# Four small edits to the order of an adaLN block: the MLP gate's sum and turn, b2's place, one pair's maxima, one group order

## The chip, the cores and the metric

The kernel runs on one core of a Trainium2 chip. The time is device microseconds of one execution; a measurement is the median of several executions. A profile is one more execution, recorded by the hardware profiler; its times are microseconds from the first instruction, and a line such as L1149 is a line of the kernel before the change. Engines are called by the names of the profile: PE (TensorE), DVE (VectorE), ACT (ScalarE), POOL (GpSimd) and SP (SyncE, which here only issues DMAs).

## What is computed

A transformer block on 2048 rows of 640 numbers, whose two halves are scaled, shifted and gated by six rows `mod` that are made from one vector `c`:

```python
mod = (silu(c) @ w_mod).reshape(1, 6, 1, 640)
sa, ca, ga, sb, cb, gb = (mod[:, i] for i in range(6))
h = layernorm(x) * (1 + ca) + sa
x = x + ga * attention(h)            # linear attention, 32 heads of 20, feature map softmax(pq), softmax(-pq)
h = layernorm(x) * (1 + cb) + sb
x = x + gb * (relu(h @ w1 + b1) ** 2 @ w2 + b2)
```

In attention each head's q and k go through a 20 x 20 matrix and two softmaxes (one of the values, one of their negatives); `kv` and `z` are sums over all rows, and the output is `phi_q kv / phi_q z`, times `wo`. The row `gb`, the MLP's gate, and its product with `b2` are what one of the edits touches.

## The kernel before, in words

The 2048 rows are 16 tiles of 128, or 8 pairs. Three stages follow each other. The first (to about 250 us) makes q, k and v of all tiles, the sums `kv` and `z`, and, on the side, the rows of `mod`. The second (about 250 to 389 us) is a loop over the 8 pairs, `for j in range(NB)`, and makes the attention's output; the sixth column of `mod`, the gate `gb`, is finished in it. The third (from 389 us) is the MLP, again pair by pair (`j`) and in seven steps (`n`) of two feature blocks (`f`).

Products are split in high and low parts: `hi` is a copy on ACT that rounds, the low part is the rest, subtracted on DVE (helper `lo`, L88), and a product is three matmuls, high by high, high by low, low by high (helper `three`, called by `mm`, L78).

The order of the second stage is written out by hand for PE, DVE, ACT and POOL (`tc.manual_schedule`): on each of these engines instructions stand in the order in which the code issues them. The order of SP's DMAs is left to the scheduler in this stage; in the MLP's first pair it is written by hand too. In one turn `j` of the second stage:

- `e_prod`, `e_recip` and `e_scale` (L877 to L906) make the scaled features of the tiles 2j+5 and 2j+6, or nearly so: two long DVE products with a sum between them, and small steps on POOL and DVE.
- `do_wo(j, i, h)` (PE tiles `pwo`) multiplies the output of pair j, in high and low parts `ot`, by `wo`: for each of two tiles (i) and two column ranges (h, 384 and 256 wide) 16 matmuls, of which the third is the first that reads a low part.
- `tr_e(j + 1, gs)` (PE `te`, ACT `ept`) transposes the features of the next pair in six groups: 0 to 4 of 120 columns in two halves, 5 of 80 columns. They go in two calls, groups 0, 1, 2 and then 5, 3, 4; `te_at` says at which of the turn's three places. The PSUM tiles of these groups and of `numa` and `numb` rotate over three banks; the five `ept` buffers are copied to by ACT.
- `num(j + 1)` (PE `numa`, `numb`, `numc`) makes the next pair's output, `num_hi` (ACT, L950) its high parts, `num_lo` its low parts; from the third pair on those are four subtractions on DVE straight from PSUM.
- Four tiles of q are postponed. In turns 1, 3 and 5 `q_chain(..., False)` makes their maxima and minima and subtracts them (two reductions `mxq`, L430 and L431, two subtractions `eq`, L433, on DVE), and `exps` (L436, L437) takes the exponentials on ACT. In turns 1 and 3 both stand after the low parts.
- At the end of turn 3 `mod_sum(5, gate_b)` (L310, DVE) sums the gate's column out of the tile `mt5`, which gives `gate_b`, 128 partitions by 5; `spread_row` (L328, L329) writes it to memory turned, one number of 4 bytes at a time, and reads it back as one row of 640 to all 128 partitions (`gb_b`).
- In turn 5 DVE makes `bb = b2 * gate` (L1149) from `b2s`, one of five rotating rows `s1`, into which `biases` (L510) loaded b2 in the stage before.
- From turn 5 on weights for the MLP are split (`p_hi`, L1014, on ACT; `p_lo` on DVE) and loaded ahead (`p_load`, L1004 and L1007, on SP, into the rotating rows `s1`).

In the MLP a step issues, for two feature blocks, `up` (PE, then ReLU on ACT, L1250, and the square on DVE, L1251), `split_a` (high and low parts `ra`), and between them `down` of the step before (PE `acc`, `acc3x`). `prep` does weight splits and loads; `add_bias` first reads `bb` in step 6 of the first pair, and `by_gate` first reads `gb_b` in the second pair.

Of the kernel before, what the change touches and what calls it, by code (L numbers as in the profile page):

```python
# [51 lines left out]
def kernel(  # L52
# [64 lines left out]
    def row(tag, name):  # L117
        return (pc if tag in ("s3", "s4") else mem).tile([P, D], F32, tag=tag, name=name, bufs=BUFS[tag])
# [347 lines left out]
    def q_chain(t, whole=True):  # L466
        if t < KEPT:
            EQ[t] = tok2(f"q{t % 2}", f"eq{t}")
        e = EQ[t]
        spread(PQ[t], e, f"q{t}")  # L470
        if whole:
            exps(e)
            q_sums(t)
# [29 lines left out]
            nc.gpsimd.dma_start(w[2 * n : m, 0], w[2 * n : m, 1])  # L503

    ga_b = row("s4", "ga_b")
    b2s = []

    def biases():
        b2s.append(row("s1", "b2s"))
        nc.sync.dma_start(b2s[0], bass.AP(tensor=b2.tensor, offset=b2.offset, ap=[[0, P], [1, D]]))  # L510

    GB = []

# [19 lines left out]
    }  # L533
    gate_a = const.tile([P, NC], F32, name="gate_a")
    gate_b = const.tile([P, NC], F32, name="gate_b")
    LAST_COL = {7: (2, gate_a), 9: (3, cols_b[:, 0:5]), 11: (4, cols_b[:, 5:10])}
    SIDE = {
        2: lambda: mod_mac(2, 0, 1, 2),
# [544 lines left out]
    def t2(j, *ds):  # L1083
        if 0 in ds:
            H2[j] = ht(f"h2_{j}", j, (0, 96))
        if j == 0:
            t_unit(XM[j], cols_b, H2[j], ds[0], f"b{j}", bank(f"tb{j}_{ds[0]}"))
            return
        p = tp(f"tb{j}_{ds[0]}")
        for k, d in enumerate(ds):  # L1090
            t_in(XM[j], d, p[:, 256 * k : 256 * k + 256])
        for k, d in enumerate(ds):
            t_out(cols_b, H2[j], d, f"b{j}", p[:, 256 * k : 256 * k + 256], XX[j][d % 2][:, :256])
# [40 lines left out]
    for j in range(NB):  # L1134
        nxt = j + 1 < NB
        b, c = 2 * j + 5, 2 * j + 6
        te_at = (0, 1) if 0 < j < 6 else (1, 2)
        if j == 4:
            load_x1(0)
        if j < 5:  # L1140
            p_load()
        if j != 5:
            e_prod(b)
        e_recip(b - 1)
        e_scale(b - 1)
        if j == 5:
            q_chain(KEPT + 3, False)
            add_x(0, 0, 1)
            nc.vector.tensor_tensor(bb, b2s[0], gb_b, op=ALU.mult)  # L1149
            ln0 = ln_parts(XM[0], "b0")  # L1150
        load_e(b + 2)
        def te(at):
            for i, gs in enumerate((range(3), (5, 3, 4))):
                if nxt and te_at[i] == at:
                    tr_e(j + 1, gs)

        do_wo(j, 0, 0)
        te(0)
        if j == 5:
            exps(EQ[KEPT + 3])  # L1160
            q_sums(KEPT + 3)
            e_prod(b)
        do_wo(j, 0, 1)
        if j == 7:
            t2(0, 0)
            t2(0, 1)
        te(1)
        if j == 5 or j == 6:
            next(ln0)
        if j in SUMS:  # L1170
            q_sums(KEPT + SUMS[j])
        e_prod(c)
        if j != 5:
            e_recip(b)
            e_scale(b)
        do_wo(j, 1, 0)
        if j == 7:
            t2(0, 2)
            t2(0, 3)
        te(2)  # L1180
        if nxt:
            num(j + 1)
            num_hi(j + 1)
        do_wo(j, 1, 1, 0, 8)
        if j == 7:
            t2(0, 4)
        if not nxt:
            do_wo(j, 1, 1, 8, 16)
        if nxt:
            do_wo(j, 1, 1, 8, 11)  # L1190
            num_lo(j + 1)
            do_wo(j, 1, 1, 11, 16)
        if j == 5:
            e_recip(b)
            e_scale(b)
        if j in SPREAD:
            q_chain(KEPT + SPREAD[j], False)
            exps(EQ[KEPT + SPREAD[j]])
        if j == 3:
            mod_sum(5, gate_b)  # L1200
            spread_row(1, gate_b, gb_b)
        load_e(c + 2)
        if j == 5:
            next(ln0)
        if 1 <= j < 6:
            p_hi()
        if j == 5:
            p_lo(4)
            p_load(4)
        if j == 6:  # L1210
            p_hi(4)
            p_lo(5)
            p_load(3)
        if j == 7:
            p_load(2)
# [315 lines left out]
    for j in range(NB):  # L1531
        if j <= PLAIN:
            if j:
                by_hand.__exit__(None, None, None)
            by_hand = tc.manual_schedule(engines={ET_.PE, ET_.DVE, ET_.Activation, ET_.Pool} | ({ET_.SP} if j != 1 else set()))
            by_hand.__enter__()
        for n in range(NP):
            down = lambda k: prev and (down_plain if plain(*prev) else down_pair)(*prev, k)
            twice = not plain(j, n)
            m = NP * j + n - NP - 1  # L1540
            if (j, n) == (NB - 1, NP - 1):
                for k in range(2):
                    up(j, 2 * n + k)
                    split_a(j, n, (k,))
                for i in range(2):
                    add(Y[j][i], Y[j][i], XR[j, i])
                break
            done = j - 1 if j and prev else None
            up(j, 2 * n)
            if prev and not plain(*prev):  # L1550
                split_s(*prev)
            down(0)
            if j < PLAIN:
                layer(j + 1, 2 * n, None if j else 0)
            if 0 < m < NP - 2:
                t_split(m - 1)
            if m == -1:
                t_load(0)
            if (j, n) == (PLAIN, 0):
                t_fetch(4)  # L1560
            if j >= PLAIN:
                if n == 5 + (j == PLAIN):
                    for i in range(2):
                        add_bias(j, i)
                layer(j + 1, 2 * n)
            prep(next(PREPS, 0))
            if j == 0:
                layer(j + 1, 2 * n, 1)
            if n == 0 and j:
                if j - 1 >= PLAIN:  # L1570
                    first_combos(j - 1)
                else:
                    Y[j - 1] = [row("s2", f"y{j - 1}_{i}") for i in range(2)]
                for r, i, c in (("3", 0, R), ("2", 0, L)):
                    end(j - 1, r, i, c)
            if n == 1 and j:
                gate(j - 1, 0)
                if j != PLAIN:
                    finish(j - 1, j < PLAIN)
            if n == 1 and j == PLAIN:  # L1580
                finish(j - 1, 0)
            if n == 2 and j == PLAIN:
                t_sums(NP - 2)
            if n == (2 if j > PLAIN else 1) and j:
                gate(j - 1, 1)
            if n == (5, 5, 5, 3)[min(j, 3)]:
                residual(j)
            for i in range(2):
                if n == 6 and j == 0:
                    add_bias(j, i)  # L1590
            if j == NB - 1 and n == 1:
                for k in range(NP - LAST, NP - 1):
                    plain_load(k)
            if j == NB - 1 and n == 3:
                for k in range(NP - LAST, NP - 1):
                    plain_split(k)
            if j == NB - 1 and n == NP - 2:
                for i in range(2):
                    by_gate(Y[j][i], Y[j][i], slice(0, D))
            up(j, 2 * n + 1)  # L1600
            if j >= PLAIN and n == 0:
                down(1)
            split_a(j, n)
            if twice:
                sums(j, n)
            if j < PLAIN or n:
                down(1)
            if m == NP + 1:
                t_split(NP - 2)
            ahead = (j, n) == (0, 3)  # L1610
            if ahead:
                layer(j + 1, 2 * n + 1)
            prep(next(PREPS, 0))
            if n == 0 and j:
                end(j - 1, "4", 1, L)
                end(j - 1, "x", 1, R)
            if n == (2 if j > PLAIN else 1 if j == PLAIN else 0) and j:
                finish(j - 1, j >= PLAIN)
            if not ahead:
                layer(j + 1, 2 * n + 1)  # L1620
            if 0 <= m < NP - 2:
                t_sums(m)
            if m == NP - 2:
                t_split(m - 1)
            if 0 < m + 1 < NP - 1:
                t_load(m + 1)
            if m == NP - 1:
                for i in range(2):
                    add_bias(j - 1, i)
            if j == NB - 1 and n == NP - LAST:  # L1630
                first_combos(j)
            prev = j, n
# [60 lines left out]
```

## Time and profile before

| | |
|---|---|
| median of 3 runs | 769.13 us (768.96 to 769.65) |
| the profiled execution's own time | 769.86 us |
| its span, first to last instruction | 768.2 us |
| granted TensorE clock | 1.000 |
| DVE busy | 593.8 us (77%) |
| ACT busy | 434.6 us (57%) |
| POOL busy | 144.2 us (19%) |

The span begins with the first instruction and ends with the last; 1.7 us of the execution's time lie around it. A timeline row shows a start, a duration, the engine and line, and the tiles written and read (`out<-in`), with the number of instructions that were merged; a bracket holds the engine's idle time before it and what ended it. Matmuls overlap one another, so that PE counts as busy through short gaps between them; the distance from one start to the next tells more than the durations.

### The profile page before, as it was taken

How to read it: one execution, taken by the hardware profiler on the slowest of the kernel's cores; microseconds unless marked ns; L12 is line 12 of the kernel's file. 1: busy time of each engine (PE TensorE's matmuls, PEld its weight loads, DVE VectorE, ACT ScalarE, POOL GpSimd, SP SyncE). 2: the span in 40 equal slices, each digit the busy share in tenths (PEclk: the TensorE clock that was granted, in tenths of full speed). 3: DMA queues.
4: the chain of work that ended last, by engine and by line, in shares of the span. 5: the costliest groups of instructions: out<-in, count | busy, mean ns of one | idle time of the engine just before them, and what ended most of it. 6: DMA issues, size and time to landing. Idle time of an engine off the chain costs nothing.

```text
span 768.2 us, 15300 instructions
## 1 busy us (share of the span) xinstructions
PE 759.3 (99%) x5967; PEld 739.8 (96%) x5967; DVE 593.8 (77%) x1083; ACT 434.6 (57%) x971; POOL 144.2 (19%) x301
## 2 busy tenths in 40 slices
PE   9999999999999999999999999999999999999997
PEld 8999999999999989888999999999999999999996
DVE  6598897989999999999565667866767666675666
ACT  5766756767843454545776647465553636445331
POOL 3001101101100255442101000231321313222110
PEclk9999999999999999999999999999999999999999
DMA  9811431343333344155356367996766758766450
GB/s 327 305 65 73 137 103 54 104 139 114 119 104 109 117 142 170 70 80 160 107 180 222 110 226 253 286 323 195 226 181 197 232 177 262 221 184 192 130 165 35
DMA packets 52151, 126.69 MB, mean 165 GB/s; under 512 B 7335, under 2 KB 8103, under 8 KB 52079
## 3 DMA queue, kind: packets, MB, share of 16 engines
q1 hardware_dynamic: 34744, 84.65, 33.1%
q0 software_dynamic: 14752, 35.76, 16.7%
q10 hardware_dynamic: 2583, 5.30, 1.8%
q8 instruction: 47, 0.77, 0.4%
q14 instruction: 25, 0.20, 0.1%
HBM read 95.70 MB, written 29.89 MB: 163 GB/s over the span
## 4 chain that ended last, share of the span: by engine, by line
PE 85%; DVE 8%; issue 2%; DMA 2%; POOL 2%; ACT 1%; SPq 0%; POOLq 0%; DVEq 0%
PE up L78 23%; PE acc L78 17%; PE pk L78 9%; PE pv L78 9%; PE pq L78 8%; PE pwo L78 5%; PE acc3x L78 5%; PE kvp L450 3%; DVE dn L879 2%; DVE scr L877 2%; DVE ezb L901 1%; PE tb L357 1%; PE te L921 1%; DMA ring_b<-td_b 1%; PE ta L357 1%
## 5 line engine op out<-in xcount | busy, mean ns | idle before, releaser
L78 PE MATMUL up<-h,w 128*128 128x256 f32 x1640 | 206.4, 278 | 0.0
L78 PEld LDWEIGHTS up<-h,w 128*128 128x128 f32 x1640 | 196.1, 188 | 0.0
L1250 ACT ACTIVATE ft<-up,b_t 128x256 f32<-128x256 f32 x104 | 48.9, 470 | 115.1 <-PE up L78 114.6
L78 PE MATMUL acc<-w,ra 128*128 128x384 f32 x452 | 97.4, 335 | 0.0
L1251 DVE TENSOR_TENSOR ft<-ft 128x256 f32<-128x256 f32 x104 | 44.1, 424 | 51.2 <-ACT ft L1250 49.6
L78 PE MATMUL pwo<-wo,ot 128*128 128x256 f32 (+3 forms) x512 | 80.8, 312 | 0.6 <-DVE ot L88 0.6
L78 PEld LDWEIGHTS pwo<-wo,ot 128*128 128x128 f32 (+1 forms) x512 | 74.5, 188 | 3.8 <-issue 2.7
L78 PE MATMUL pq<-wq,hT 128*128 128x384 f32 (+1 forms) x480 | 75.2, 312 | 0.0
L78 PEld LDWEIGHTS acc<-w,ra 128*128 128x128 f32 x452 | 72.7, 188 | 0.7 <-DVE ra L88 0.5
L78 PE MATMUL pk<-wk,hT 128*128 128x384 f32 (+1 forms) x480 | 72.7, 308 | 0.0
L78 PE MATMUL pv<-wv,hT 128*128 128x384 f32 (+1 forms) x480 | 71.7, 307 | 0.0
L78 PEld LDWEIGHTS pq<-wq,hT 128*128 128x128 f32 x480 | 71.1, 188 | 0.6 <-issue 0.2
L78 PEld LDWEIGHTS pk<-wk,hT 128*128 128x128 f32 x480 | 70.5, 188 | 0.4 <-issue 0.2
L78 PEld LDWEIGHTS pv<-wv,hT 128*128 128x128 f32 x480 | 70.1, 188 | 0.0
L88 DVE TENSOR_TENSOR ra<-ft,ra 128x384 fp32r<-128x384 f32 (+2 forms) x86 | 36.8, 448 | 32.9 <-ACT ra L1274 20.2
L78 PE MATMUL acc3x<-w,ra 128*128 128x256 f32 x248 | 42.3, 278 | 1.4 <-DVE end L1418 1.4
L1360 POOL DMA_DIRECT2D ring_a<-td_a x34 | 18.3, 537 | 125.5 <-PE acc L78 103.2
L1274 ACT ACTIVATE ra<-ft 128x384 fp32r<-128x384 f32 x48 | 25.2, 526 | 28.4 <-DVE ft L1251 22.4
L78 PEld LDWEIGHTS acc3x<-w,ra 128*128 128x128 f32 x248 | 39.5, 188 | 1.8 <-DVE end L1418 1.6
L1265 DVE TENSOR_TENSOR ft<-ft 128x128 f32<-128x128 f32 x136 | 33.3, 286 | 1.2
L441 DVE TENSOR_REDUCE sk<-ek 128x64 f32<-128x1280 f32 x16 | 23.7, 1484 | 12.4 <-ACT ek L436 10.8
L885 POOL TENSOR_TENSOR dn<-dn,rs_q 128x32 f32<-128x32 f32 x32 | 20.1, 629 | 68.1 <-DVE dn L879 67.8
(264 smaller groups left out, 1406.5 us busy)
## 6 DMA issues: line engine op xcount, KB each, us to landing
ring_c<-td_c POOLq DMA_DIRECT2D x34, 384.0 KB, 4.0
ring_a<-td_a POOLq DMA_DIRECT2D x34, 384.0 KB, 4.1
ring_b<-td_b POOLq DMA_DIRECT2D x34, 256.0 KB, 4.0
esp<-eq SPq DMA_DIRECT2D x12, 640.0 KB, 3.2
el<-esp SPq DMA_DIRECT2D x12, 640.0 KB, 4.0
rw<-in_w SPq DMA_DIRECT2D x23, 320.0 KB, 3.1
wm<-in_w_mod SPq DMA_DIRECT2D x20, 320.0 KB, 3.7
xb<-in_x SPq DMA_DIRECT2D x8, 640.0 KB, 4.0
```

Of the source, the lines that this page charges most:

```text
L78: nc.tensor.matmul(o, a, b, start=first and i == 0, stop=last and i == len(terms) - 1, skip_group_check=skip,)
L88: (eng or nc.vector).tensor_tensor(out_lo, full, hi.bitcast(F32), op=ALU.subtract)
L357: nc.tensor.transpose(p[:, i * P : (i + 1) * P], xn[:, i, d * P : (d + 1) * P], ident)
L441: nc.vector.tensor_reduce(s, heads(flat(e)), axis=AX.X, op=ALU.add)
L450: nc.tensor.matmul(kvp[g // 4][64 * c : 64 * c + 64, a : a + 2 * n].rearrange("p (s n) -> p s n", s=2), v[:, u], e[:, :, o : o + n], start ...
L877: nc.vector.tensor_tensor(z, flat(ET[t]), flat(zb), op=ALU.mult)
L885: nc.gpsimd.tensor_tensor(dn[:, s], dn[:, s], rs[:, 1 - s], op=ALU.mult)
L1250: nc.scalar.activation(r, p, AF.Relu, bias=b1_t[:, f : f + 1])
L1251: nc.vector.tensor_tensor(r, r, r, op=ALU.mult)
L1265: nc.vector.tensor_tensor(t[:, o], t[:, a], t[:, b], op=op)
L1274: nc.scalar.activation(a[:, 0, :3], t[:, :3], AF.Copy)
L1360: nc.gpsimd.dma_start(RING[j, n, r], TD[n][r].bitcast(F32R))
```

## The change

Four things are edited.

1. The gate. Its sum moves from the end of turn 3 to turn 6, behind `e_scale`. The column is no longer turned by 4-byte writes: in turn 7 PE transposes `gate_b` to 5 partitions by 128 in a PSUM tile, ACT copies it to `gate_r`, and SP writes it to memory in five rows of 512 bytes and reads it back to all partitions.
2. b2 is loaded straight into `bb`, and the product with the gate is made in place, in step 4 of the MLP's first pair in place of turn 5.
3. In turn 1 the maxima of the postponed tile (`q_chain`) stand ahead of the pair's low parts, behind `e_scale`; its exponentials stay where they were.
4. Where the second call of `tr_e` comes early in the turn (turns 1 to 5), its groups go 3, 4, 5 in place of 5, 3, 4.

```diff
     def biases():
-        b2s.append(row("s1", "b2s"))
-        nc.sync.dma_start(b2s[0], bass.AP(tensor=b2.tensor, offset=b2.offset, ap=[[0, P], [1, D]]))
+        nc.sync.dma_start(bb, bass.AP(tensor=b2.tensor, offset=b2.offset, ap=[[0, P], [1, D]]))
...
+    gate_r = pc.tile([NC, P], F32, name="gate_r")
...
         e_scale(b - 1)
+        if j == 6:
+            mod_sum(5, gate_b)
         if j == 5:
             q_chain(KEPT + 3, False)
             add_x(0, 0, 1)
-            nc.vector.tensor_tensor(bb, b2s[0], gb_b, op=ALU.mult)
             ln0 = ln_parts(XM[0], "b0")
...
-            for i, gs in enumerate((range(3), (5, 3, 4))):
+            for i, gs in enumerate((range(3), (3, 4, 5) if te_at[0] == 0 else (5, 3, 4))):
...
             e_recip(b)
             e_scale(b)
+        if j == 1:
+            q_chain(KEPT + SPREAD[j], False)
         do_wo(j, 1, 0)
...
         if j == 7:
             t2(0, 4)
+            p = tp("gbt")[:NC, :P]
+            nc.tensor.transpose(p, gate_b, ident)
+            nc.scalar.activation(gate_r, p, AF.Copy)
+            nc.sync.dma_start(GD[1], gate_r)
+            nc.sync.dma_start(gb_b, GD[1].rearrange("c p -> (c p)")[None, :].to_broadcast([P, D]))
...
         if j in SPREAD:
-            q_chain(KEPT + SPREAD[j], False)
+            if j > 1:
+                q_chain(KEPT + SPREAD[j], False)
             exps(EQ[KEPT + SPREAD[j]])
-        if j == 3:
-            mod_sum(5, gate_b)
-            spread_row(1, gate_b, gb_b)
...
+            if (j, n) == (0, 4):
+                nc.vector.tensor_tensor(bb, bb, gb_b, op=ALU.mult)
```

More of the change, by code (lines that the diff above doesn't have):

```diff
@@ L505 @@
     ga_b = row("s4", "ga_b")
-    b2s = []
     def biases():
-        b2s.append(row("s1", "b2s"))
-        nc.sync.dma_start(b2s[0], bass.AP(tensor=b2.tensor, offset=b2.offset, ap=[[0, P], [1, D]]))
+        nc.sync.dma_start(bb, bass.AP(tensor=b2.tensor, offset=b2.offset, ap=[[0, P], [1, D]]))
     GB = []
```

## The prediction

> **What bounds the kernel now.** I read the page first, then the waits of PE, then PE's timeline of the second stage, then DVE and ACT beside it.
>
> ```profile
> span 768.2 us, 15300 instructions
> PE 759.3 (99%) x5967; PEld 739.8 (96%) x5967; DVE 593.8 (77%) x1083; ACT 434.6 (57%) x971; POOL 144.2 (19%) x301
> ```
> ```profile
> PE acc L78 <- DMA ring_b<-td_b: 0.7, 1, 0.7
> PE pwo L78 <- DVE ot L88: 0.6, 1, 0.6
> PE te L921 <- ACT ept L923: 0.3, 1, 0.3
> ```
>
> PE is busy for 759.3 of 768.2 us, so only what shortens or lengthens PE's own row counts. In the part that is edited PE has two recorded waits, the last two rows: one for the low part `ot`, one for an `ept` copy (the first row is the MLP's). As matmuls overlap, each costs more than the wait shown. The distances of starts tell how much:
>
> ```profile
> 301.40 4.89 PE L78 MATMUL pwo<-wo,ot 128*128 128x256 f32 x32
> 306.12 1.48 PE L921 MATMUL te<-ident,ezb 128*120 128x128 f32 x12
> 307.36 2.13 PE L78 MATMUL pwo<-wo,ot 128*128 128x256 f32 x16
> 309.82 1.63 PE L921 MATMUL te<-ident,ezb 128*80 128x128 f32 x10 [0.33 <-ACT ept L923]
> 311.20 3.02 PE L78 MATMUL pwo<-wo,ot 128*128 128x384 f32 x16
> ...
> 316.89 3.33 PE L78 MATMUL pwo<-wo,ot 128*128 128x256 f32 x22
> ```
> ```profile
> 321.81 1.47 PE L921 MATMUL te<-ident,ezb 128*120 128x128 f32 x12
> 323.04 2.08 PE L78 MATMUL pwo<-wo,ot 128*128 128x256 f32 x16
> ...
> 325.98 3.08 PE L78 MATMUL pwo<-wo,ot 128*128 128x384 f32 x16
> ```
> ```profile
> 346.52 2.46 PE L78 MATMUL pwo<-wo,ot 128*128 128x256 f32 x18
> 349.55 0.61 PE L78 MATMUL pwo<-wo,ot 128*128 128x384 f32 x2 [0.57 <-DVE ot L88]
> ```
> ```profile
> 352.11 1.47 PE L921 MATMUL te<-ident,ezb 128*120 128x128 f32 x12
> ```
>
> The same 16 narrow matmuls and 10 transposes take 311.20 - 307.36 = 3.84 us in turn 2 and 325.98 - 323.04 = 2.94 us in turn 3: the wait for `ept` costs 0.90 us. The 32 `pwo` matmuls from a turn's end to its first `te` take 306.12 - 301.40 = 4.72 us without a wait, 321.81 - 316.89 = 4.92 us at the next turn and 352.11 - 346.52 = 5.59 us at the one with the wait for `ot`: 0.20 and 0.87 us lost. So 1.97 us in all is what these edits can give back on PE, a quarter of a per cent. **The gain has a ceiling of some 2 us, before anything is paid.**
>
> **The second pair's maxima.** Who is late, and why, stands on DVE and ACT:
>
> ```profile
> 301.78 0.68 DVE L88 TENSOR_TENSOR ot<-numa,ot 128x512 fp32r<-128x512 f32 x1
> ...
> 303.64 0.80 DVE L430 TENSOR_REDUCE mxq<-eq 128x32 f32<-128x640 f32 x1
> ...
> 306.80 1.48 DVE L877 TENSOR_TENSOR scr<-el,zb 128x1280 f32<-128x1280 f32 x1
> ```
> ```profile
> 306.91 0.74 ACT L436 ACTIVATE eq<-eq 128x640 f32<-128x640 f32 x1 [2.99 <-DVE eq L433]
> ```
> ```profile
> 311.45 2.77 PE pwo L78 x16
> ```
>
> DVE is not idle at the place: the low parts begin as soon as `e_scale` is out, at 301.78. They take 303.64 - 301.78 = 1.86 us, the chain of maxima 306.80 - 303.64 = 3.16 us. ACT waits 2.99 us for the chain before the exponentials, and the `ept` copies that PE waits for at 309.82 stand behind these. With the chain first, the exponentials begin about 1.9 us sooner and that 0.90 us goes. But the first low part then ends at 301.78 + 3.16 + 0.68 = 305.62. PE needs it in the third wide matmul: 16 of them take 2.77 us (0.173 each, from the chain of work), they end at 306.12, so the first starts at 303.35 and the third at 303.70. In the wait that is there now, the low part of `numa` ends at 349.50 and PE goes on at 349.55:
>
> ```profile
> 331.19 0.69 DVE L88 TENSOR_TENSOR ot<-numa,ot 128x512 fp32r<-128x512 f32 x1 [0.42 <-ACT ot L950]
> ...
> 336.37 0.81 DVE L310 TENSOR_REDUCE gate_b<-mt 128x5 f32<-128x640 f32 x1
> 337.10 1.48 DVE L877 TENSOR_TENSOR scr<-eq,zb 128x1280 f32<-128x1280 f32 x1
> ...
> 348.82 0.68 DVE L88 TENSOR_TENSOR ot<-numa,ot 128x512 fp32r<-128x512 f32 x1
> ```
>
> So 0.05 us from DVE to PE; and of the 0.87 us lost there, the late start is 349.55 - (346.52 + 2.30) = 0.73, the restart 0.14. Here PE goes on at 305.67: 1.97 us late, with the restart **+2.11 us**. The later low parts come 0.6 us apart and are read half a microsecond apart or more; they add nothing. DVE's own work is only permuted: it reaches `scr` at 306.80 as before. Then back: **-0.90** at `ept`, and **-0.20** at the next pair's low part, which DVE delivers at its old time to a PE that is now 1.2 us later. PE stands at +1.01.
>
> **The sum of the gate, turn 3.** The reduction holds DVE for 337.10 - 336.37 = 0.73 us, between the third postponed tile's maxima and the work whose end is the low part at 348.82. DVE has waited just before, for ACT and so for PE (0.42 us at 331.19). Hence DVE's chain from there starts with PE at +1.01 and loses 0.73: the low part is ready at 349.50 + 0.28, and PE, which without a wait would be there at 348.82 + 1.01 = 349.83, goes on at that moment. It had gone on at 349.55: **PE is at +0.28** behind this pair. What mattered before as a wait of 0.87 us pays for most of the rest. The reduction's new place in turn 6 lies in a hole of DVE:
>
> ```profile
> 375.79 0.69 DVE L88 TENSOR_TENSOR ot<-numa,ot 128x512 fp32r<-128x512 f32 x1 [5.75 <-ACT ot L950]
> ```
>
> 5.75 us idle hide 0.73; without that cover it would come on the next low parts. Turn 5 loses the product L1149, but PE waits for nothing there: nothing.
>
> **The group order.** Group 5 has 80 columns against twice 120 of the others; the sixth group of a pair takes the `ept` buffer that `num`'s first matmuls free. With 5 as the sixth the copy is shorter, and `num` reads it last. PE waits for none of this outside the wait that is counted already: between nothing and -0.15 us; I take nothing.
>
> **The turn by transpose.** One transpose on PE, behind two others, so that the change of kind is paid: 12 take 1.31 us in the chain, one **+0.11**. ACT's copy of 5 partitions lies ahead of the MLP's first ReLU. SP gets two DMAs, the second waits for the first to land, and weight loads are queued behind:
>
> ```profile
> 392.90 0.33 SPq L1004 DMA_DIRECT2D rw<-in_w  x1
> ```
> ```profile
> x<-xm SPq DMA_DIRECT2D x6, 320.0 KB, 2.3
> ...
> gate<-gate_b SPq DMA_DIRECT2D x1, 2.5 KB, 11.5
> ```
> ```profile
> 390.92 0.47 ACT L1250 ACTIVATE ft<-up,b_t 128x256 f32<-128x256 f32 x1 [0.78 <-PE up L78]
> ...
> 396.45 1.36 ACT L1014 ACTIVATE w<-rw 128x640 fp32r<-128x640 f32 x2
> 398.15 0.47 ACT L1250 ACTIVATE ft<-up,b_t 128x256 f32<-128x256 f32 x1 [0.34 <-PE up L78]
> ```
>
> ACT falls idle at 390.92 - 0.78 = 390.14, so the copy is hidden and `gate_r` is ready at about 390.4 (an estimate from this row and PE's shift). Between 2.3 us (a store of whole rows) and 11.5 us (the same 2.5 KB in 4-byte pieces) to land, the second DMA goes at 392.7 or 401.9. The load at 392.90 (the second to be split at 396.45, so at 397.1) follows 0.4 us later. At 2.3 us it stays where it was. I take this end, as five rows of 512 bytes are nearer to rows than to pieces; the other end is a rival. [...]
>
> **b2's product in the MLP.** The product sits between a weight's low part and the square of the second feature block:
>
> ```profile
> 357.50 0.82 DVE L1149 TENSOR_TENSOR bb<-b2s,gb_b 128x640 f32<-128x640 f32 x1
> 358.24 1.48 DVE L478 TENSOR_REDUCE rs_q<-eq 128x64 f32<-128x1280 f32 x1
> ```
> ```profile
> 419.42 0.83 DVE L88 TENSOR_TENSOR w<-rw,w 128x640 fp32r<-128x640 f32 x1 [0.16 <-ACT w L1014]
> 420.59 0.43 DVE L1251 TENSOR_TENSOR ft<-ft 128x256 f32<-128x256 f32 x1 [0.34 <-ACT ft L1250]
> 421.61 0.76 DVE L88 TENSOR_TENSOR ra<-ft,ra 128x384 fp32r<-128x384 f32 x2 [0.59 <-ACT ra L1274]
> ```
> ```profile
> 418.47 0.68 PE L78 MATMUL acc<-w,ra 128*128 128x384 f32 x3
> ...
> 421.89 0.78 PE L78 MATMUL acc<-w,ra 128*128 128x384 f32 x3
> ```
>
> DVE has 0.34 us of idle there, the product holds it 358.24 - 357.50 = 0.74 us. The square moves from 420.59 to 419.42 + 0.74 + 0.74 = 420.90, and with it ACT's high and DVE's low part. PE's third `acc` matmul at 421.89 + 0.34 reads that low part when it has just come (0.78 us for three, 0.68 in the group before): no slack. **+0.31 us.** Ends: nothing, if ACT's backlog there is shorter behind a later PE, and 0.74. b2's direct load waits for no row; loads wait for none now that PE feels: nothing, and at most as much either way as the MLP's one DMA wait of PE, 0.7 us (PE `acc` for `ring_b`), which any shift of the loads may take away or double.
>
> **Sum:** 2.11 - 0.90 - 0.20 - 0.73 + 0.11 + 0.31 = +0.70 us on the profiled execution's 769.86 (span 768.2 and 1.7 around it). That one lies 0.73 above the median of 769.13, so I forecast the median: **769.8 us**.
>
> **Rivals.**
> - *The chain doesn't hold the low parts*, because the issued order stays the old one, or because DVE is done earlier in turn 1. Then 2.11 isn't paid, the `ept` wait stays or goes, and the gain is between 0.87 and 1.97, less 0.11 and 0.31: 767.6 to 768.7. Against it: the order on DVE is written by hand, and DVE has no idle before 301.78. 11%.
> - *Nothing is paid back.* PE's 2.11 stay, as the `ept` copies or the low part come late again behind a later PE: 2.11 + 0.42 = 2.53, or 1.6 if one of the two comes back: 770.8 to 771.7. For it: PE is later by a microsecond wherever DVE or ACT wait for it. 17%.
> - *SP stands behind the gate's round trip* (slower). At 11.5 us the weight load goes at 402.3 in place of 392.9 and lands 2.3 us later or more, at 404.6, 7.5 us after ACT wants to split it; the split stands ahead of a ReLU, PE's `down` behind that. ACT's idle of 0.34 us absorbs a little: +7 us with the forecast's other terms, 777. It decides from the point where the load lands after 397.4, a landing of the gate in 4.3 us. 5%.
> - *The MLP's DMA wait shifts*, by 0.7 us either way, on top of the forecast: 769.1 or 770.5. 12%.
>
> The forecast itself, 769.3 to 770.4, has 55%. A difference of 0.2%, 1.5 us, is about what a measurement of this kernel can tell from no change: below 767.6 is faster, above 770.7 slower. Faster gets part of the first rival and of a lucky DMA, 7%; slower nearly all of the second, the third, and some of the forecast's upper edge with an unlucky DMA, 27%; within, 66%. The range for 8 in 10 goes from the upper half of the first rival to most of the second: 768.2 to 771.5.
>
> **What would show it.** Right: PE waits once some 2 us for `ot` near 303.7 with `mxq` ahead of the low parts on DVE; the waits at 309.8 and 349.55 are gone; the first pair after that is less than half a microsecond late; L1149's successor stands ahead of a square, and PE's `acc` there loses 0.3 us. Wrong: no wait near 303.7; a wait for `ept` still; DMA landing of the gate over 4 us; a new wait of PE at the MLP's start.

## The result, and the profile after

| | before | after |
|---|---|---|
| median | 769.26 us (768.87 to 770.81, 22 executions) | 771.37 us (769.77 to 774.15, 22 executions) |
| ratio after / before | | 1.0023 [1.0016, 1.0031] |
| the profiled execution's own time | 769.86 us | 769.77 us |
| its span | 768.2 us | 768.0 us |

The change makes the kernel slower by 0.23%. That lies inside the predicted range of 768.2 to 771.5, close to its upper end; the forecast of 769.8 us is 1.6 us too low. The table holds a riddle: the profiled execution of after is no slower than that of before, while the median is 2.1 us higher. The spread shows why to be careful: 4.4 us between the extremes of after, 1.9 us of before.

The head of the page of the kernel after, and below it the waits of PE between 250 and 450 us, the part of the span that was edited (columns: total, times, longest, in us):

```profile
span 768.0 us, 15305 instructions
PE 759.0 (99%) x5968; PEld 739.7 (96%) x5968; DVE 594.0 (77%) x1083; ACT 435.7 (57%) x972; POOL 144.6 (19%) x301
```
```profile
PE pwo L78 <- DVE ot L88: 1.9, 1, 1.9
```

PE has one instruction more, the transpose. Of its two waits in this part both are gone, the 0.6 us for `ot` at 349.55 and the 0.3 us for `ept` at 309.82, and a single one of 1.9 us has come. PE's timeline of after shows it with its place:

```profile
301.12 2.44 PE L78 MATMUL pwo<-wo,ot 128*128 128x256 f32 x18
305.49 2.70 PE L78 MATMUL pwo<-wo,ot 128*128 128x384 f32 x14 [1.92 <-DVE ot L88]
308.02 1.47 PE L920 MATMUL te<-ident,ezb 128*120 128x128 f32 x12
309.25 2.08 PE L78 MATMUL pwo<-wo,ot 128*128 128x256 f32 x16
311.17 1.25 PE L920 MATMUL te<-ident,ezb 128*120 128x128 f32 x10
312.19 3.08 PE L78 MATMUL pwo<-wo,ot 128*128 128x384 f32 x16
```

DVE and ACT of after, at the same place:

```profile
301.58 0.81 DVE L430 TENSOR_REDUCE mxq<-eq 128x32 f32<-128x640 f32 x1
302.31 0.80 DVE L431 TENSOR_REDUCE mxq<-eq 128x32 f32<-128x640 f32 x1
303.15 1.68 DVE L433 TENSOR_TENSOR eq<-eq,mxq 128x640 f32<-128x640 f32 x2
304.75 0.68 DVE L88 TENSOR_TENSOR ot<-numa,ot 128x512 fp32r<-128x512 f32 x1
...
306.61 1.47 DVE L876 TENSOR_TENSOR scr<-el,zb 128x1280 f32<-128x1280 f32 x1
```
```profile
304.87 0.74 ACT L436 ACTIVATE eq<-eq 128x640 f32<-128x640 f32 x1 [1.23 <-DVE eq L433]
```

The chain of maxima holds DVE from 301.58 to 304.75 (3.17 us), and the first low part ends at 305.43. PE does the 16 narrow matmuls and the two wide ones that need high parts only, stands idle from 301.12 + 2.44 = 303.56 to 305.49, and goes on 0.06 us after the low part. ACT's exponentials begin at 304.87 in place of 306.91, so that the ten `te` run without a hole from 311.17.

The later places, in PE's timeline of after: two pair beginnings, and the transpose of the gate.

```profile
317.94 4.89 PE L78 MATMUL pwo<-wo,ot 128*128 128x256 f32 x32
322.67 1.48 PE L920 MATMUL te<-ident,ezb 128*120 128x128 f32 x12
...
347.23 5.17 PE L78 MATMUL pwo<-wo,ot 128*128 128x256 f32 x32
352.25 1.48 PE L920 MATMUL te<-ident,ezb 128*120 128x128 f32 x12
...
388.19 0.27 PE L1190 MATMUL gbt<-ident,gate_b 128*5 128x128 f32 x1
388.22 1.18 PE L78 MATMUL pwo<-wo,ot 128*128 128x256 f32 x8
```

No bracket stands in them; the 32 matmuls behind 347.23 still take 352.25 - 347.23 = 5.02 us against 4.72 undisturbed, so PE meets the low part at the moment when it comes. SP's DMAs of the gate in after, and the product with b2 on DVE with PE's `acc` behind it:

```profile
390.18 0.28 SPq L1192 DMA_DIRECT2D gate<-gate_r  x1
391.37 0.33 SPq L1193 DMA_DIRECT2D gb_b<-gate  x1
393.14 0.33 SPq L1003 DMA_DIRECT2D rw<-in_w  x1
```
```profile
420.38 0.82 DVE L1575 TENSOR_TENSOR bb<-bb,gb_b 128x640 f32<-128x640 f32 x1
421.12 0.42 DVE L1256 TENSOR_TENSOR ft<-ft 128x256 f32<-128x256 f32 x1
```
```profile
422.15 1.04 PE L78 MATMUL acc<-w,ra 128*128 128x384 f32 x3
```

The weight load behind the gate goes at 393.14 (392.90 before). The square follows the product at 421.12, and the three `acc` take 1.04 us in place of 0.78.

**Where did 2.1 us come from, if the profile doesn't have them?** The distances between starts of PE, against those of before, make a sum: 301.12 to 308.02 is 6.90 against 4.72 (+2.18); to 312.19 it is 4.17 against 5.08 (-0.91); to 322.67, 10.48 against 10.61 (-0.13); to 352.25, 29.58 against 30.30 (-0.72). Behind it +0.11 around the transpose (from 352.25 to 388.22; 352.11 to 387.97 before) and 1.04 - 0.78 = +0.26 at `acc`: **+0.79 us**. This profiled execution hides them: PE stands 0.28 us earlier in it already at 301.12, ahead of all edits but the row into which b2 is loaded, and PE's wait of 0.7 us for `ring_b` in the MLP is missing from it; 0.79 - 0.28 - 0.7 = -0.2, the difference of the spans. So 0.8 us are explained; 1.3 of the 2.1 are not in this trace at all.

The times of all executions show the rest, with the mean granted clock of each beside them. A mean of 0.998 or less is taken as a fall of the clock within the kernel; 0.999 needs none (in the kernel without part 3, below, the clock falls at 766.67, behind PE's last matmul, 1.6 us before the span ends, and its mean is 0.999). Of the 33 executions of after (22, and 11 of a second series below), 14 have a clock of 0.999 or 1.000 and a median of 770.05 us, 0.8 above before's 769.26; 19 have 0.998 or less and a median of 771.82. Among 94 executions of before, run beside the experiments, not one lies under 0.999 (their median is 769.24).

### The profile page after: what moved, and what is told of

The parts are those of the page before. It is cut to its first block, busy times and chain, and to the rows that moved or that the text cites. A ratio compares the mean times of both kernels' runs of the same rounds, so it can differ in the third digit from the quotient of the medians.

```text
span 768.0 us, 15305 instructions
## 1 busy us (share of the span) xinstructions
PE 759.0 (99%) x5968; PEld 739.7 (96%) x5968; DVE 594.0 (77%) x1083; ACT 435.7 (57%) x972; POOL 144.6 (19%) x301
## 4 chain that ended last, share of the span: by engine, by line
PE 90%; DVE 3%; DMA 3%; issue 2%; ACT 1%; POOL 1%; SPq 0%; POOLq 0%; DVEq 0%; ACTq 0%
PE up L78 21%; PE acc L78 16%; PE pwo L78 9%; PE pq L78 9%; PE pk L78 9%; PE pv L78 9%; PE acc3x L78 4%; PE kvp L450 3%; PE te L920 2%; PE tb L357 1%; DMA raw_q<-in_wq 1%; PE numa L78 1%; DMA ring_b<-td_b 1%; PE ta L357 1%; PE numc L78 1%
```

## The experiments

The theory (in the expectations CLOCK): in the wait near 303.5 PE stands idle long enough that, in a part of the executions, the chip takes its clock back for a while, and the matmuls behind the wait are slow. Rivals: that the price is in the waits alone, or in some other edit. The first four kernels, which ran on the same chip, take the edit out, make it alone, fill the wait, and repeat.

**The change without part 3.** The maxima of turn 1 go back behind the low parts:

```diff
-        if j == 1:
-            q_chain(KEPT + SPREAD[j], False)
         do_wo(j, 1, 0)
...
-            if j > 1:
-                q_chain(KEPT + SPREAD[j], False)
+            q_chain(KEPT + SPREAD[j], False)
```

> The changed kernel with the second pair's maxima put back behind the low parts; the gate, b2 and the group order stay changed. Theory CLOCK (the 1.9 us wait of PE near 303.7 lets the granted clock fall in most executions, and that, not the sum of waits, makes the median): no wait near 303.7, clock 1.000 in every execution, a spread as narrow as before's, and a time of before less 0.9 (the low part behind the gate's sum) plus 0.1 (transpose) plus 0.3 (b2's product): 768.3 to 769.2. Rival GATE (the new round trip of the gate, or b2's product, makes the executions differ): 770.5 to 772 with the same spread of 4 us and clocks below 1. Rival ORDER (the group order costs): a wait for ept longer than before's 0.3 us.

Measured: 769.42 us (11 executions), 0.2 us above the expected range, ratio to before 1.0000 [0.9992, 1.0009]; no execution under 0.999. PE's only wait between 250 and 450 us in it:

```profile
PE te L920 <- ACT ept L922: 0.4, 1, 0.4
```

So PE again waits for `ept`, as before, and not for `ot`. That it is 0.4 us and not 0.3 was to be the sign of the rival ORDER; but the distance of starts there is shorter, 310.97 - 306.08 = 4.89 us against 5.08, and the next pair's low part takes that back (5.08 against 4.92). Two rows of PE's timeline of this kernel give the gain of the gate's sum, and one the cost of b2's product:

```profile
301.37 4.87 PE L78 MATMUL pwo<-wo,ot 128*128 128x256 f32 x32
...
351.35 1.48 PE L920 MATMUL te<-ident,ezb 128*120 128x128 f32 x12
...
421.25 1.04 PE L78 MATMUL acc<-w,ra 128*128 128x384 f32 x3
```

351.35 - 301.37 = 49.98 us against 50.71 before: -0.73, the time for which the reduction held DVE (the last experiment, with the same second stage, has -0.62). With +0.11 and +0.26 that is -0.36. The median lies 0.3 above before's 769.16 of that series; the interval reaches down to -0.6, so the two agree, but the gain isn't measured by the time, only by the trace.

**Part 3 alone,** made on the kernel before (the same edit the other way round):

```diff
+        if j == 1:
+            q_chain(KEPT + SPREAD[j], False)
         do_wo(j, 1, 0)
...
-            q_chain(KEPT + SPREAD[j], False)
+            if j > 1:
+                q_chain(KEPT + SPREAD[j], False)
```

> The kernel before with the second pair's maxima ahead of the low parts and nothing else. CLOCK: the wait of 1.9 us is there, so are clocks below 1.000 in more than half of the executions; PE pays 2.1, gets 0.9 and 0.2 back and has nothing from the gate's sum: +1.0 by waits, +1.5 to 2 by the clock, 771.3 to 772.3, spread of 3 to 4 us. Rivals GATE and ORDER: +1.0 alone, 769.9 to 770.5, spread of before.

Measured: 771.94 us (9), ratio 1.0032 [1.0022, 1.0043]; 6 of 9 at 0.998, their median 772.5. This one part makes the whole loss and more.

**The wait filled.** Eleven superfluous matmuls, overwritten by the ones behind them, go ahead of the waiting group:

```diff
+        if (t, h, a) == (4, 0, 0):
+            for _ in range(11):
+                nc.tensor.matmul(PWO[t][0][:, :384], WO[0][:, 0, :P], WO[0][:, 0, :384], start=True, stop=True)
```

> The changed kernel with 11 more matmuls (128 x 384, 0.173 us each, 1.9 us) ahead of the waiting group, into the PSUM tile that this group overwrites: the same order and the same lateness of the low part, but PE works through it. CLOCK: clock 1.000 in every execution, spread of before, before plus 0.5 to 0.9: 769.6 to 770.2. Rivals GATE and ORDER: nothing changes against the changed kernel, 771 to 772 with its spread.

Measured: 770.86 us (12), ratio 1.0018 [1.0009, 1.0027]; no execution under 0.999. PE's timeline of it:

```profile
303.62 2.08 PE L976 MATMUL pwo<-wo 128*128 128x384 f32 x11
305.54 3.24 PE L78 MATMUL pwo<-wo,ot 128*128 128x384 f32 x16
308.61 1.47 PE L920 MATMUL te<-ident,ezb 128*120 128x128 f32 x12
```

From this pair's first matmul (301.69) to 308.61 it is 6.92 us, as in after (6.90): PE is as late as with the wait, but it isn't idle, and the clock doesn't fall. The median, though, is 0.9 us above before's 769.16 with the 0.8 us of the waits, and above the expected range; see what stays open.

**After, once more,** to have the count of executions and, with luck, a profile with a fall.

> The changed kernel unchanged, for more executions and another profile beside the three above. CLOCK: medians of 770.8 to 772; executions at clock 1.000 lie near 769.8 and each 0.001 of the mean clock lost costs about 1 us; before's executions all at 1.000. If the profile falls into an execution with a lower clock, the slices after 303 us show it and those before do not. Rivals: times and clocks do not go together, or before has lower clocks too.

Measured: 771.55 us (11), ratio 1.0025 [1.0015, 1.0034]; 7 of 11 at 0.998 or less, the profiled one among them. PE's timeline of it, and the windows view (columns: stretch, its length, PE busy with its instructions, granted clock, DMA share, GB/s) of this execution and, last, of after's first:

```profile
305.41 4.27 PE L78 MATMUL pwo<-wo,ot 128*128 128x384 f32 x14 [1.94 <-DVE ot L88]
309.52 1.48 PE L920 MATMUL te<-ident,ezb 128*120 128x128 f32 x12
```
```profile
302.00:305.50 3.50, 1.56 (x13) 1.00 0.80 263
305.50:309.00 3.50, 3.50 (x12) 0.53 0.06 21
309.00:312.50 3.50, 3.50 (x31) 0.98 0.00 0
```
```profile
302.00:305.50 3.50, 1.58 (x14) 1.00 0.76 261
305.50:309.00 3.50, 3.50 (x23) 1.00 0.06 22
```

Same kernel, same wait; but the 14 matmuls behind it take 309.52 - 305.41 = 4.11 us against 308.02 - 305.49 = 2.53, **1.58 us more**, with 12 instructions in the stretch in place of 23 at a clock of 0.53. The "busy" column says 3.50 of 3.50 both times: a slow PE is as busy as a fast one. The records of the granted clock in this trace: 1.0 from 5.36 to 305.74, 0.5 for 3.413 us, then 1.0 again.

Why only some executions? In these traces the lengths between the clock's changes are whole multiples of 3.413 us: 224 of them, 764.585 us, at full clock in the profiles of before and of after, 88 of them, 300.37 us, here. I read that as a raster on which the clock is set. Its phase against the kernel differs: full clock begins in the records at 4.51 us in before's profile, at 4.21 in after's, at 5.36 here. It can be counted where the raster cut the wait:

| execution | idle of PE | raster cuts it at | longest idle inside one window | clock behind it |
|---|---|---|---|---|
| after | 303.56 to 305.49 | 304.58 | 1.02 | 1.0 |
| after, once more | 303.48 to 305.41 | not (302.32 to 305.74) | 1.93 | 0.5 for 3.41 us |
| part 3 alone | 304.16 to 306.00 | not (303.75 to 307.17) | 1.84 | 0.5 for 3.41 us |

From this came the second theory: what counts is the idle time inside one window of the raster, with a limit somewhere between 1.0 and 1.8 us. The 1.6 us of the expectations is an estimate that fits the falls so far: if all phases are equally frequent, one window holds 1.6 us or more of a wait of 1.93 us in (3.413 + 1.93 - 2 x 1.6) / 3.413 = 63% of them, and 25 of 42 executions, 60%, have a fall. Its rival (ANY): that any new wait at this place does it. Two kernels with a shorter and a longer wait, on one chip.

**A shorter wait.** One of the two subtractions of the chain goes back behind the low parts:

```diff
         if j == 1:
-            q_chain(KEPT + SPREAD[j], False)
+            tq = KEPT + SPREAD[j]
+            eq, pq = EQ[tq], PQ[tq]
+            mxq = small([P, 2, H], "mx", f"mxq{tq}")
+            nc.vector.tensor_reduce(mxq[:, 0], heads(pq), axis=AX.X, op=ALU.max)
+            nc.vector.tensor_reduce(mxq[:, 1], heads(pq), axis=AX.X, op=ALU.min)
+            nc.vector.tensor_tensor(heads(eq[:, 1]), heads(pq), over(mxq[:, 1]), op=ALU.subtract)
...
+            if j == 1:
+                nc.vector.tensor_tensor(heads(eq[:, 0]), heads(pq), over(mxq[:, 0]), op=ALU.subtract)
```

> The changed kernel with only both reductions and one of the two subtractions ahead of the low parts, the other behind: PE's wait near 303.7 is 0.8 us shorter, 1.1 us. Theory CLOCK in its window form (the record shows drops of exactly 3.413 us at places of a free-running raster; a window that holds more than some 1.6 us of idle PE makes the next one run at half clock): no drop in any execution, since 1.1 us can't fill that; clocks 0.999 to 1.000, PE +2.1 - 0.8 and most of the 0.9 at ept back, before plus 0 to 0.8: 769.0 to 770.0. Rival ANY (any late start of PE of about a microsecond lowers the clock, with a chance that grows with its length): clocks of 0.998 in a third of the executions, 770 to 771.

Measured: 769.58 us (11), ratio 1.0001 [0.9992, 1.0010]; none under 0.999. PE's row and the stretch behind it:

```profile
305.03 2.71 PE L78 MATMUL pwo<-wo,ot 128*128 128x384 f32 x14 [1.02 <-DVE ot L88]
```
```profile
302.00:305.50 3.50, 2.48 (x20) 1.00 0.64 208
305.50:309.00 3.50, 3.50 (x26) 1.00 0.20 76
```

Here the whole 1.02 us lie in one window (303.66 to 307.07), and the clock stays: not every wait does it.

**A longer wait.** One reduction is made twice:

```diff
         if j == 1:
+            mxq = small([P, 2, H], "mx", "again")
+            nc.vector.tensor_reduce(mxq[:, 0], heads(PQ[KEPT + 1]), axis=AX.X, op=ALU.max)
             q_chain(KEPT + SPREAD[j], False)
```

> The changed kernel with one of the reductions made twice, so that PE waits 0.73 us longer, 2.65 us. CLOCK with a window: drops of 3.413 us in about 80% of the executions (60% at 1.9 us): of a raster of 3.41 us the places where one window holds 1.6 us or more of the wait are 3.41 + 2.65 - 2 x 1.6 long; by waits before plus 1.2 to 1.5 as the rest of DVE's work comes later too, with the drop 772.0 to 773.0. ANY: nearly all executions, more than one drop, 773 or more. If the clock has nothing to do with the wait: drops as seldom as before, 770.3.

Measured: 771.96 us (12), ratio 1.0029 [1.0019, 1.0040]; 7 of 12 at 0.998 or less, fewer than expected, though with 12 executions that can't be told from either share. The profiled one is at 0.994; its windows:

```profile
302.00:305.50 3.50, 1.45 (x12) 0.99 0.82 271
305.50:309.00 3.50, 2.94 (x9) 0.50 0.03 12
309.00:312.50 3.50, 3.50 (x16) 0.53 0.00 0
```

The raster cuts the wait (303.45 to 306.06) at 305.45, so that 2.00 us lie in one window. Two windows at half clock follow; 0.61 us of the wait lie in the first of them. Whether that makes the second wasn't tried.

The count over all kernels:

| PE's wait at this place | executions | clock at 0.998 or less |
|---|---|---|
| 2.6 us | 12 | 7 |
| 1.8 to 1.9 us (after twice, part 3 alone) | 42 | 25 |
| 1.0 us | 11 | 0 |
| filled with matmuls (two series) | 23 | 0 |
| none (the other five experiments) | 56 | 0 |
| none (before) | 94 | 0 |

So the wait lowers the clock: the falls come with it, go when it is taken out, shortened or filled, and are there when it alone is added.

**The filled wait again,** for the time that it has too much.

> The kernel of e3_filled once more, because its median lay 0.6 above its sum of waits though its clock never dropped. If that was chance: 769.6 to 770.4. If the eleven matmuls cost something besides, which its profile did not show: 770.5 to 771.2 again, clocks of 0.999 to 1.000.

Measured: 770.71 us (11), ratio 1.0013 [1.0005, 1.0022], again none under 0.999, and again too slow by its median: by 0.6 us against before's 769.28 of that series and the 0.8. But the intervals of the two series are 0.7 to 2.1 us and 0.4 to 1.7 us above before, and 0.8 lies in both, so an extra cost isn't shown.

**The gain without the wait.** Can the 0.9 us at `ept` be had another way? The maxima go back, and the exponentials of turn 1 are issued in turn 2, behind the `ept` copies; b2's product moves to step 2 of the MLP:

```diff
         te(0)
+        if j == 2:
+            exps(EQ[KEPT + 1])
...
-            exps(EQ[KEPT + SPREAD[j]])
+            if j != 1:
+                exps(EQ[KEPT + SPREAD[j]])
...
-            if (j, n) == (0, 4):
+            if (j, n) == (0, 2):
                 nc.vector.tensor_tensor(bb, bb, gb_b, op=ALU.mult)
```

> The changed kernel with the second pair's maxima back behind the low parts, their exponentials issued a turn later, behind the copies of the first three groups, and b2's product in step 2 of the MLP's first pair, where DVE idles 1.2 us. By waits: no wait at ept (-0.9), none at the low part behind the gate's sum (-0.87), plus 0.11 for the transpose, nothing for b2: -1.5 us in PE's alignment up to the MLP's fifth step, clock 1.000; the median 767.3 to 768.3 if the MLP's DMA waits stay as they are. If these take up what PE comes earlier: 768.5 to 769.2, with waits of PE for ring_a or ring_b that are longer by the difference.

Measured: 768.65 us (12), ratio 0.9993 [0.9985, 1.0002]; and the same kernel in a later series:

> The kernel of e7_exps_later once more, to narrow its interval: 0.9993 again by theory DVE (0.7 won in the second stage, 0.1 paid), 0.998 by the sum of the waits.

768.81 us (11), ratio 0.9997 [0.9988, 1.0006]. The sum of the waits expected more. The medians lie in the expectation's other range, 768.5 to 769.2, but not for its reason, longer DMA waits in the MLP. PE's timeline of the first of the two:

```profile
301.62 4.87 PE L78 MATMUL pwo<-wo,ot 128*128 128x256 f32 x32
...
316.25 2.46 PE L78 MATMUL pwo<-wo,ot 128*128 128x256 f32 x18
319.50 1.66 PE L78 MATMUL pwo<-wo,ot 128*128 128x384 f32 x8 [0.79 <-DVE ot L88]
```

From 301.62 to 316.25 it is 14.63 us against 15.49 before: the 0.9 are won. Three microseconds later PE waits 0.79 us for the next pair's low part. DVE hasn't become faster, so what PE wins at one place it waits for at the next. That suggests that DVE sets the pace in this stretch, however busy PE looks; the next experiment asks it.

**Work taken from DVE there.** The same kernel, with the sums of the postponed tile (`rs_q`, a reduction of 1.47 us on DVE) made one turn later:

```diff
-    SPREAD, SUMS = {1: 1, 3: 2}, {2: 1, 4: 2}
+    SPREAD, SUMS = {1: 1, 3: 2}, {3: 1, 4: 2}
```

> The kernel of e7_exps_later, and the sums of that postponed tile (one DVE reduction of 1.4 us) a turn later, behind the low part that e7 saw late. Theory DVE (between 276 and 349 us DVE is the bound and PE's waits only move from one place to the next; what counts is the work that DVE loses, 0.73 us of the gate's sum, and its idle of 0.4 us near 331): no wait near 319, a shorter one behind the gate's old place instead, and PE behind it 1.1 us ahead of before's row where e7 was 0.7 us ahead; before less 1.0, ratio 0.9985 to 0.999. Rival PE (the waits are separate): all of 0.9 and 0.87 stay won, 1.7 us ahead, ratio 0.998.

Measured: 767.89 us (11), ratio **0.9985 [0.9976, 0.9993]**, span 765.9 us: faster than both kernels. It has no wait of PE between 250 and 450 us. Its timeline:

```profile
300.88 4.87 PE L78 MATMUL pwo<-wo,ot 128*128 128x256 f32 x32
...
315.51 4.89 PE L78 MATMUL pwo<-wo,ot 128*128 128x256 f32 x32
320.24 1.48 PE L920 MATMUL te<-ident,ezb 128*120 128x128 f32 x12
...
345.12 5.31 PE L78 MATMUL pwo<-wo,ot 128*128 128x256 f32 x32
350.27 1.47 PE L920 MATMUL te<-ident,ezb 128*120 128x128 f32 x12
```

350.27 - 300.88 = 49.39 us against 50.71: 1.3 us less, 0.6 of it since the kernel before this one (351.65 - 301.62 = 50.03). The 0.79 don't come back (320.24 - 315.51 = 4.73, the undisturbed distance), DVE's idle of 0.19 and 0.24 us near 331 is gone, and behind 345.12 the low part still costs 350.27 - 345.12 = 5.15 against 4.72. That, and the ratio, are about as the theory DVE had it (1.1 us); the rival PE expected 1.7 us.

**b2's product in step 2,** without part 3 and with nothing else:

```diff
-            if (j, n) == (0, 4):
+            if (j, n) == (0, 2):
                 nc.vector.tensor_tensor(bb, bb, gb_b, op=ALU.mult)
```

> The kernel of e1_no_maxima (the second pair's maxima and exponentials where they were before) with b2's product in step 2 of the MLP's first pair in place of step 4. If the product's place costs what the alignment of PE showed (0.26 us at 422) and nothing else is in it: no step of PE at 422, and 0.7 us less in the second stage plus 0.1 for the transpose: before less 0.6, ratio 0.9990 to 0.9996; the wait for ept of 0.3 to 0.4 us is there. If e1's ratio of 1.0 is made by something else of the gate's new way: 1.0 again.

Measured: 769.11 us (11), ratio 0.9990 [0.9981, 0.9999], at the edge of the expected range. The group of `acc` that the product had delayed, in PE's timeline:

```profile
421.49 0.78 PE L78 MATMUL acc<-w,ra 128*128 128x384 f32 x3
```

0.78 us, as in the kernel before, against 1.04: the place of the product cost 0.26 us, and in step 2 it costs nothing there.

## Why the prediction was right, and where it failed

- **The low part near 303.7:** +2.11 predicted, +2.18 measured, and the mechanism as told, PE going on 0.06 us behind DVE (0.05 predicted).
- **What is paid back:** `ept` -0.90 predicted, -0.91 measured; the next pair's low part -0.20 and -0.13; the gate's sum -0.73 and -0.72. The low part near 350 ends as the race that was foretold, with PE 0.42 us late behind it (0.28 predicted). The gate's sum is shown without part 3 too (-0.73).
- **The gate's sum in turn 6** stands at 369.83 on DVE, in a hole, and costs nothing. **The group order** was taken at nothing; it wasn't tried by itself. In the kernel without part 3 it may be what shortens PE's row at `ept` by 0.19 us, which the next pair takes back.
- **The transpose:** +0.11 and +0.11. A price for the change of kind isn't shown: in before, 12 `te` between two groups of `pwo` take 307.36 - 306.12 = 1.24 us from their first start to that of the next `pwo`, no more than the 1.31 of the chain. **b2's product:** +0.31 and +0.26, and its place is shown as the cause by the last experiment.
- **The gate's round trip:** the second DMA goes 391.37 - 390.18 = 1.19 us after the first, faster than either of the two bounds (2.3 and 11.5). The rival that SP stands behind it is refuted. The price of the 4-byte pieces, 11.5 us, is gone, but the lower bound, taken from a store of 320 KB, was too high for 2.5 KB. No run tells the size of the pieces, 4 bytes against 512, from their number, 640 against 5.
- **The sum by waits:** +0.70 predicted, +0.79 measured, and +0.8 is the median of those executions of after whose clock didn't fall (a selection; see what stays open).

**The step that failed** is "Here PE goes on at 305.67: 1.97 us late, with the restart +2.11 us". The wait is sized well, but its price doesn't end with the first matmul behind it: in 19 of 33 executions the clock falls, in the profiled one of these to half for one window, and that costs another 1.58 us there (1.77 between the two medians). As that is more than half of the executions, the median moves with it: 0.8 + 1.3. No rival named this. The rival "nothing is paid back" has the right time, 770.8 to 771.7, and the wrong reason: 1.76 us were paid back, place by place. The range reached up to 771.5 only for this rival's sake, so it was luck that the measured 771.37 lies inside; the 769.3 to 770.4 of the forecast's own mechanism missed it.

The prediction took the clock of 1.000 in the profile before as given, and its sum has no term for a fall. It belonged to the kernel before, whose waits in this part were 0.57 us at most, and the change made one of 1.92 us, three times as long. In the profiles with a fall, 1.84 to 2.00 us of idle inside one window of 3.413 us came ahead of half clock. Where the clock stayed, the sum was close to the forecast's +0.70 us: +0.79 by the trace, +0.8 by the median of the executions without a fall.

**What stays open.** First, where the limit lies. The end of the kernel narrows it, as PE falls idle inside some window of the raster there too. Two windows of the raster in the profile of before (the last matmul ends at 764.03):

```profile
762.27:765.68 3.41, 1.76 (x11) 1.00 0.27 96
765.68:768.15 2.47, 0.00 (x0) 1.00 0.21 80
```

PE is idle for 3.41 - 1.76 = 1.65 us of the first, and the clock stays at 1.00 in the second. Without part 3 that idle is 2.5 us, and the clock is 0.50 behind it. So the limit lies between 1.65 us (no fall) and 1.84 us (fall) by the profiled executions, if one rule holds at both places. PE's wait of 1.43 us near 760, which every kernel here has, fits: in before's profile it lies whole in one window, and no execution of before has a fall. An estimate from the share of falls: a wait of 1.93 us escapes if the raster cuts it so that neither part reaches the limit T, which happens in (2T - 1.93) / 3.413 of the phases, if all phases are equally frequent; 14 of 33 gives T = 1.7 us.

And the medians of the filled wait are 0.9 and 0.6 us above its waits, if that isn't chance; its trace shows no place for them. One reason may be a selection. PE stands at the beginning of this pair at 300.88 to 301.77 us in the profiles whose clock rises to 1.0 by 5.5 us (median 301.12 of seven), at 301.53 to 301.71 where it rises at 6.5 us or later (median 301.65 of six). If the theory holds, after keeps its clock when the raster cuts its wait in the middle, as in the profile whose clock rises at 4.21, so its 14 executions without a fall may be the ones that start early; the filled ones are all phases. Whether that is the difference wasn't tried. In the times, then, filling the wait isn't shown to win much; in the clocks, 0 of 23 against 19 of 33, its effect is plain.

## What to carry to other kernels

In this kernel a wait of PE had a price of its own when it neared two microseconds: with 1.8 to 1.9 us, 25 of 42 executions had a fall of the clock, in the profile of after, once more, to half for 3.41 us. So look at the clocks of all executions before you trust one profile (a mean of 0.998 over 770 us was one such window there). A wait that can't be avoided may be kept short by splitting the work that causes it: at 1.0 us none of 11 executions had a fall. In the stretch where DVE seems to set the pace, a wait that was removed (0.9 us) came back at the next meeting point (0.79 us); what brought time was to move DVE's work, the sums, to a later turn (768.65 and 768.81 us to 767.89).

## What of the hardware was not expected

- Half clock for 3.413 us (once 6.83) after an idle PE of 1.84 us and more inside one window of the raster, in three profiles, and none after 1.65 us in another; a mean clock of 0.998 or less in 32 of 54 executions with a wait of 1.8 us or more, in none of 184 others.
- A store of five rows of 512 bytes lets the next DMA go 1.19 us after its issue, where the same 2.5 KB in 4-byte pieces took 11.5 us to land.
